# A spectral filter and a gated feed-forward on one core: x of two batches and the output weights loaded as plain f32 and cast on the engines, the opening's queues in a new order

## The chip, the core and the metric

The kernel runs on one core of a Trainium2 chip. The metric is device time in microseconds, the median of several executions. The core has five engines, each with a queue of its own that it works through in order: TensorE (PE in the profile; PEld is its weight load), VectorE (DVE), ScalarE (ACT), GpSimd (POOL) and SyncE (SP), which here only issues transfers. Transfers (DMAs) issued by SP or ACT move bytes as they are; those issued by POOL can change the type on the way, and the kernel before uses that to load f32 as f16. All of them run on the same 16 DMA engines.

## The reference

x has 8 batches of 3008 positions by 256 channels. Each channel of each batch is filtered in the frequency domain, then every position goes through a normalized, gated feed-forward of width 1536:

```python
X = np.fft.rfft(x, axis=1)
Y = X * (filt_r + 1j * filt_i)[None, :, :]
y = np.fft.irfft(Y, n=x.shape[1], axis=1)          # (8, 3008, 256)
x = y.reshape(24064, 256)
xn = x / np.sqrt(np.mean(x * x, -1, keepdims=True) + 1e-6) * rms_g
g = xn @ w_gate
out = (g / (1 + np.exp(-g))) * (xn @ w_val) @ w_out
```

All inputs and the output are f32; TensorE works on f16.

## The kernel before, in words

**The filter.** 3008 is 47 times 64; the transform is done in two steps. Positions are laid out as 94 partitions by 32 rows (r). Step one (`s1`, L139) multiplies with a 94 by 96 table `w1`, two rows of r at a time, 16 times a batch; the result goes to tile `a_sb` (one for each four calls, four slots) and by a store to `a_tmp` in DRAM, from which `load_a2` (L156) fetches it in another order. Step two (`s2`, L195) multiplies with the table `u`, then with the filter: for batches 0 and 1 by two DVE products straight from psum (L207 with `fr_sb`, L208 with `fi_sb`). `s2z` (L221) transforms back by `v1` and `v2` (made on the chip by `make_v`, L452), ACT evicts to `z_sb`, and each third call stores to `z_tmp`. `load_z2` (L240) fetches that in another order into the one slot of tag `z2`. `s3` (L247) is the last transform and takes the sums of squares on ACT (`junk`, L256); `s3r` (L260) makes rho from them on POOL; `s3n` (L271) normalizes on DVE into `n_sb`, stores that, and `load_xn` fetches it transposed as `xn`.

**Batch 0** takes shorter ways, so that TensorE starts early. `s1_first` (L163) computes step one with x as the stationary operand, four groups of eight rows, and leaves the result transposed in `at`, which borrows the slot of `z2`; `turn` (L183) turns it back into `a2` on TensorE, without the trip through DRAM. The first two chunks (`PRE` = 2) of normalized rows are turned on TensorE too (`turn_n`, L294, from `s3n_first`, L282), without a trip.

**The feed-forward** runs in units (`unit`, L337): for a chunk of 376 (batch 0) or up to 512 positions and one of 12 column blocks, two gate matmuls `pg`, two value matmuls `pv`, a Silu on ACT (L349), a DVE product to `hh` (L351), and three units later the projection `po` (`project`, L354). There are 50 chunks and 600 units. The work of the filter for later batches is dealt out to slots by a plan written by hand: `at(slot, f, ...)` puts a call behind the unit of that number.

**The opening.** All calls stand under a manual schedule: each engine works in the order of the code. POOL first issues four transfers of x of batch 0 (`load_x`, L130, f32 to f16 on the way) and the first of four pieces of the filters (`load_f`, L436: each piece is four transfers, each into every second of 64 partitions, half of them rows of 6 KB and half single rows of 1 KB); SP issues the tables. In a loop over the four groups of x follow `s1_first`, `make_v`, and, on SP, the other filter pieces, held back by a DVE memset (L510) into the columns that they fill. `copy_f` (L447) copies each filter piece to the other half of the partitions, the first time with DVE for `fr_sb`, else all on POOL. Then a loop over j has `turn(j)`, `s2(0, j - 2)` and `s2z(0, j - 4)` side by side. In it SP issues the first four feed-forward weight pieces (`load_w`, L476, 256 KB f32 each, staged in tag `xn`), and POOL issues x of batch 1, folds four pieces (`fold_w`, L482: times rms_g, to f16, columns reordered) and issues the first third of the output weights (`load_wo`, L488). Behind the loop come two loads of eight rows of `z2`, four more weight pieces, 12 calls of `s1` of batch 1, `s3` and `s3r` for the first two chunks, the last four calls of `s1`, `turn_n(0)`, four folds on DVE, `turn_n(1)`, the rest of `z2` and `load_a2(1)`; then the units.

Of the kernel before, what the change touches and what calls it, by code (L numbers as in the profile page):

```python
# [13 lines left out]
ALU = mybir.AluOpType  # L14
# [9 lines left out]
RP = 32  # L24
PX = 2 * M1
PY = 96
QZ = 4 * NS
# [4 lines left out]
def _make_tables():  # L32
# [32 lines left out]
    def rows_first(a):  # L65
        a = a.reshape(NS, 4, RP, P).transpose(2, 1, 0, 3)
        return np.ascontiguousarray(a.reshape(P, NS, P)).astype(f16)

    return (w1.reshape(PX, QZ).astype(f16), rows_first(u),
            w0.reshape(P, 1).astype(np.float32), t.reshape(QZ, PY).astype(f16),  # L70
# [4 lines left out]
def kernel(  # L75
# [12 lines left out]

    w1_np, u_np, w0_np, t_np, eye_np = _make_tables()
    w1_d = nc.inline_tensor(w1_np, name="w1tab").ap()  # L90
    u_d = nc.inline_tensor(u_np, name="utab").ap()
    w0_d = nc.inline_tensor(w0_np, name="w0tab").ap()
# [18 lines left out]
    v1_sb = glob.tile([P, NS, P], FP16)  # L111
    eye_sb = work.tile([P, 512], FP16, tag="hh", name="eye", bufs=5)[:, 0:P]
    w0_sb = glob.tile([P, 1], FP32)
# [16 lines left out]
    def load_x(b):  # L130
        v = st[b]
        v.x = []
        for g in range(4):
            xt = work.tile([PX, 8, D], FP16, tag="xt", name="xt", bufs=4)
            nc.gpsimd.dma_start(
                xt, x[b].rearrange("(p r) d -> p r d", r=RP)[:, ds(8 * g, 8), :])
            v.x.append(xt)

    def s1(b, i, eng):  # L139
        v = st[b]  # L140
        if i % 4 == 0:
            v.a = work.tile([QZ, 8, D], FP16, tag="a_sb", name="a_sb", bufs=4)
        ps = bank("psa")
        nc.tensor.matmul(ps[0:QZ, :], w1_sb, v.x[i // 4][:, ds(2 * (i % 4), 2), :],  # L144
                         start=True, stop=True)
        dst = v.a[:, ds(2 * (i % 4), 2), :]
        src = ps[0:QZ, :].rearrange("p (r d) -> p r d", r=2)
        if eng == 0:
            nc.scalar.activation(out=dst, in_=src, func=AXT.Copy)  # L149
        else:  # L150
            nc.vector.tensor_copy(out=dst, in_=src)
        if i % 4 == 3:
            nc.sync.dma_start(
                a_dram[b].rearrange("s c r d -> (s c) r d")[:, ds(8 * (i // 4), 8), :], v.a)

# [7 lines left out]
    def s1_first(g):  # L163
        v = st[0]
        if g == 0:
            t1 = work.tile([P, RP, D], FP16, tag="z2", name="at", bufs=1)
            v.at = t1.rearrange("p a b -> p (a b)")[:, 0:2 * NS * P].rearrange(
                "p (h s r c) -> p h s r c", h=2, s=NS, r=RP)
            v.a2 = work.tile([P, NS, D], FP16, tag="a2", name="a2", bufs=1)
        for i in range(2):  # L170
            for dh in range(2):
                ps = bank("psa")
                for r in range(4):
                    nc.tensor.matmul(ps[:, ts(r, QZ)], v.x[g][:, 4 * i + r, ts(dh, P)], w1_sb,
                                     start=(r == 0), stop=(r == 3))
                dst = v.at[:, dh, :, ds(8 * g + 4 * i, 4), :]
                src = ps[:, 0:4 * QZ].rearrange("p (r s c) -> p s r c", r=4, s=NS)
                if dh == 0:
                    nc.scalar.activation(out=dst, in_=src, func=AXT.Copy)
                else:  # L180
                    nc.vector.tensor_copy(out=dst, in_=src)

    def turn(j):  # L183
        v = st[0]
        ps = bank("psa")
        for e in range(2):
            for dh in range(2):
                k = 2 * e + dh
                nc.tensor.matmul(ps[:, ts(k, P)],
                                 v.at[:, dh, 2 * j + e, :, :].rearrange("p r c -> p (r c)"),  # L190
                                 eye_sb, start=(k == 0), stop=(k == 3))
# [101 lines left out]

    def turn_n(c):  # L294
        n = s3n_first(c)
        xn = work.tile([P, 2, 512], FP16, tag="xn", name="xn", bufs=9)
# [26 lines left out]
    for v in st:  # L323
        v.t12, v.y, v.xn = {}, {}, {}

# [71 lines left out]
    def at(slot, f, *args):  # L397
        plan.setdefault(slot, []).append((f, args))

    for c in range(PRE, RP // 4):  # L400
        k = 2 + 8 * (c - PRE)
        at(k, s3, 0, 2 * c, 2)
# [5 lines left out]
    for b in range(1, B):  # L408
        end = FIRST + UNITS * (b - 1)
        o_s1 = 44 if b == 2 else end - 118  # L410
        o_s2, p_s2 = (12, 3) if b == 1 else (end - 75, 2)
        o_s3 = 62 if b == 1 else end - 31
        if b > 1:
# [38 lines left out]
    def make_v(c):  # L452
# [6 lines left out]
        if k:  # L459
            nc.scalar.activation(out=v1_sb[:, 0, :], in_=pv[:, 0, :], func=AXT.Copy, scale=w0_sb)  # L460
        nc.scalar.activation(out=v1_sb[:, 4 * c + k:4 * c + 4, :], in_=pv[:, k:4, :],
                             func=AXT.Copy, scale=VSCALE)
        if c % 2 == 1:
            sl = ds(4 * c - 4, 8)
            v2 = work.tile([P, 8, P], FP16, tag="u", name="v2", bufs=3)
            v2_sb.append(v2)
            nc.vector.tensor_copy(out=v2[0:64], in_=v1_sb[64:P, sl, :])
            nc.vector.tensor_scalar(out=v2[64:P], in0=v1_sb[0:64, sl, :],
                                    scalar1=-1.0, scalar2=None, op0=ALU.mult)

# [17 lines left out]
    def load_wo(k):  # L488
        nc.gpsimd.dma_start(wo_sb[:, ts(k, 4), :],
                            moe_w_out.rearrange("(k p i) d -> k p i d", p=P, i=4)[k])  # L490

    with tc.manual_schedule():
        load_x(0)
        nc.sync.dma_start(w1_sb, w1_d)
        nc.sync.dma_start(u_sb, u_d)
        nc.sync.dma_start(eye_sb, eye_d)
        nc.sync.dma_start(w0_sb, w0_d)
        nc.sync.dma_start(t_sb, t_d)
        for dh in range(2):
            nc.sync.dma_start(g_sb[:, ds(dh, 1)], moe_rms_g[ds(dh * P, P)].unsqueeze(-1))  # L500
        nc.vector.memset(half_sb, -0.5)
        load_f(0, nc.gpsimd)
        for g in range(4):
            s1_first(g)
            if g < 3:
                make_v(2 * g)
                make_v(2 * g + 1)
            if g > 0:

                nc.vector.memset(fr_sb[0:1, 6 * g, 0:1], 0.0)  # L510
                load_f(g, nc.sync)
        copy_f(0)
        for j in range(15):
            if j < 12:
# [7 lines left out]
            if j == 6:  # L522
                load_w(4)
            if j == 10:
                load_x(1)
                for i in range(4):
                    fold_w(i, nc.gpsimd)
                load_wo(0)
        s2z(0, 11)
        load_z2(0, 0, 8)  # L530
        load_z2(0, 8, 8)
        load_w(4)
        for i in range(12):
            s1(1, i, i % 2)
        for c in range(PRE):
            s3(0, 2 * c, 2)
            s3(0, 2 * c + 1, 2)
            s3r(0, 2 * c, 2)
        for i in range(12, 16):
            s1(1, i, 1)  # L540
        load_wo(1)
        load_wo(2)
        turn_n(0)
        load_w(4)
        for i in range(4, 8):
            fold_w(i, nc.vector)
        turn_n(1)
        load_z2(0, 16, 16)
        load_a2(1)
        for i in range(8, 12):  # L550
            at(5, fold_w, i, nc.vector)

# [38 lines left out]
```

## Time and profile before

| what | us |
|---|---|
| median of 3 runs (904.06 to 905.67) | 904.35 |
| the profiled execution, whole | 903.57 |
| its span, first to last instruction | 901.7 |
| first gate matmul of the first unit | 60.97 |
| TensorE busy, whole span | 862.3 (96%) |
| first / last filter product of batch 0 (L207, L208) starts | 19.43 / 33.44 |
| last z store issued / landed | 35.32 / 42.4 |
| first `psy` matmul (L250) | 49.28 |

The views used below: *busy time of stretches* has for each stretch its length, the busy time of PE, PEld, DVE, ACT and POOL (with the number of instructions), the mean granted TensorE clock, the mean busy share of the 16 DMA engines and the GB/s that they moved. The *chain of waits* follows the work that ended last back from its end, here in order of time: start, length, and what ran or was waited for. The *timeline* has start, length, engine, line, operation, output and inputs; brackets hold the idle time before and what ended it. The *DMA view* cuts a stretch into 40 slices, with the GB/s moved in each.

### The profile page before, as it was taken

How to read it: one execution, taken by the hardware profiler on the slowest of the kernel's cores; microseconds unless marked ns; L12 is line 12 of the kernel's file. 1: busy time of each engine (PE TensorE's matmuls, PEld its weight loads, DVE VectorE, ACT ScalarE, POOL GpSimd, SP SyncE). 2: the span in 40 equal slices, each digit the busy share in tenths (PEclk: the TensorE clock that was granted, in tenths of full speed). 3: DMA queues.
4: the chain of work that ended last, by engine and by line, in shares of the span. 5: the costliest groups of instructions: out<-in, count | busy, mean ns of one | idle time of the engine just before them, and what ended most of it. 6: DMA issues, size and time to landing. Idle time of an engine off the chain costs nothing.

```text
span 901.7 us, 16399 instructions
## 1 busy us (share of the span) xinstructions
PE 862.3 (96%) x5528; PEld 549.6 (61%) x5528; DVE 645.6 (72%) x1025; ACT 640.1 (71%) x1455; POOL 336.5 (37%) x438
## 2 busy tenths in 40 slices
PE   5659999999999999999999999999999999999997
PEld 4326766666556655666556665566656665665655
DVE  4658887895588947697477965789477985865554
ACT  5546678777886778677886878867786775854543
POOL 3712104592245803285044821459033850500000
PEclk9859999999999999999999999999999999999999
DMA  9995766565436565354645554365653425260101
GB/s 211 238 257 124 167 156 212 122 145 130 144 101 143 128 146 170 99 108 129 163 146 129 138 123 151 106 131 145 146 159 100 97 78 117 77 130 24 42 29 45
DMA packets 140796, 117.30 MB, mean 130 GB/s; under 512 B 53960, under 2 KB 125256, under 8 KB 140712
## 3 DMA queue, kind: packets, MB, share of 16 engines
q1 hardware_dynamic: 136472, 102.36, 42.5%
q0 software_dynamic: 4240, 13.90, 8.6%
q8 instruction: 43, 0.70, 0.3%
q14 instruction: 41, 0.34, 0.1%
HBM read 56.96 MB, written 60.42 MB: 130 GB/s over the span
## 4 chain that ended last, share of the span: by engine, by line
PE 87%; ACT 4%; DMA 3%; DVE 2%; issue 2%; POOL 1%; ACTq 0%; SPq 0%; DVEq 0%; POOLq 0%
PE po L364 26%; PE pv L346 26%; PE pg L342 25%; PE psy L250 2%; PE psa L144 2%; ACT junk L256 2%; PE psz L229 2%; PE psp L200 2%; ACT sg L349 2%; DMA fi_sb<-in_filt_i_dram 1%; DMA z_tmp<-z_sb 1%; DMA z<-z_tmp 1%; DVE t L208 1%; DVE hh L351 0%; POOL fi_sb L450 0%
## 5 line engine op out<-in xcount | busy, mean ns | idle before, releaser
L351 DVE TENSOR_TENSOR hh<-pv,sg 128x512 f16<-128x512 f32 (+2 forms) x600 | 392.5, 658 | 219.8 <-ACT sg L349 128.3
L349 ACT ACTIVATE sg<-pg 128x512 f32<-128x512 f32 (+2 forms) x600 | 340.6, 568 | 193.8 <-PE pg L342 159.9
L364 PE MATMUL po<-wo_sb,hh 128*128 128x256 f16 (+2 forms) x2304 | 349.4, 272 | 0.2 <-DVE n_sb L276 0.2
L346 PE MATMUL pv<-xn,wv_sb 128*128 128x512 f16 (+2 forms) x1200 | 342.2, 367 | 4.4 <-ACT sg L349 3.8
L342 PE MATMUL pg<-xn,wg_sb 128*128 128x512 f16 (+2 forms) x1200 | 342.4, 367 | 0.6 <-DVE wg_sb L484 0.3
L364 PEld LDWEIGHTS <-hh 128*128 128x128 f16 (+2 forms) x2304 | 235.0, 104 | 102.4 <-DVE n_sb L276 0.5
L346 PEld LDWEIGHTS <-wv_sb 128*128 128x128 f16 x1200 | 117.5, 98 | 132.7 <-issue 6.3
L265 POOL TENSOR_SCALAR me<-ms 96x2 f32<-96x2 f32 (+1 forms) x120 | 26.0, 217 | 349.3 <-ACT junk L256 348.4
L342 PEld LDWEIGHTS <-wg_sb 128*128 128x128 f16 x1200 | 117.4, 98 | 14.1 <-issue 1.1
L217 POOL TENSOR_TENSOR pi<-pi,fi_sb 64x512 f32<-64x512 f32 x72 | 91.3, 1268 | 70.4 <-ACT pi L214 66.6
L256 ACT ACTIVATE junk<-psy 96x256 f16<-96x256 f32 x256 | 97.1, 379 | 20.9 <-PE psy L250 8.7
L218 POOL TENSOR_TENSOR qq<-pr,pi 128x512 f16<-128x512 f32 x72 | 91.6, 1272 | 10.2 <-DVE pi L216 4.4
L267 POOL TENSOR_TENSOR rho<-me,half_sb 96x2 f32<-96x2 f32 (+1 forms) x120 | 87.3, 728 | 10.0
L276 DVE TENSOR_TENSOR n_sb<-psy,rho 96x512 f16<-96x512 f32 x112 | 75.8, 677 | 0.0
L234 ACT ACTIVATE z_sb<-psz 128x512 f16<-128x512 f32 x96 | 57.3, 597 | 10.1 <-PE psz L232 5.8
L149 ACT ACTIVATE a_sb<-psa 96x512 f16<-96x512 f32 x94 | 55.4, 591 | 7.2 <-PE psa L144 3.5
L250 PE MATMUL psy<-z,t_sb 96*96 96x512 f16 x128 | 49.2, 389 | 7.8 <-DMA z<-z_tmp 7.8
L216 DVE TENSOR_TENSOR pi<-psp,fi_sb 64x512 f32<-64x512 f32 x72 | 49.9, 693 | 1.9
L215 DVE TENSOR_TENSOR pr<-psp,fr_sb 128x512 f32<-128x512 f32 x72 | 49.6, 689 | 0.6
L256 ACT ACTIVATION_READ_ACCUMULATOR junk<-psy 96x1 f32 x256 | 49.0, 191 | 0.0
L214 ACT ACTIVATE pi<-psp 64x512 f32<-64x512 f32 x72 | 42.4, 588 | 6.1
L144 PE MATMUL psa<-xt,w_sb 94*96 94x512 f16 x112 | 42.5, 399 | 3.0 <-DMA xt<-in_x_dram 2.8
(53 smaller groups left out, 382.6 us busy)
## 6 DMA issues: line engine op xcount, KB each, us to landing
out_dram<-o SPq DMA_DIRECT2D x70, 256.0 KB, 2.5
z_tmp<-z_sb SPq DMA_DIRECT2D x32, 384.0 KB, 2.3
xt<-in_x_dram POOLq DMA_DIRECT2D x32, 376.0 KB, 7.3
a_tmp<-a_sb SPq DMA_DIRECT2D x28, 384.0 KB, 3.6
a<-a_tmp SPq DMA_DIRECT2D x28, 384.0 KB, 5.5
z<-z_tmp SPq DMA_DIRECT2D x7, 1536.0 KB, 10.0
n_tmp<-n_sb SPq DMA_DIRECT2D x28, 384.0 KB, 3.0
out_dram<-o SPq DMA_DIRECT2D x14, 224.0 KB, 2.6
```

The costliest lines, as they stand in the source:

```text
L144: nc.tensor.matmul(ps[0:QZ, :], w1_sb, v.x[i // 4][:, ds(2 * (i % 4), 2), :], start=True, stop=True)
L217: nc.gpsimd.tensor_tensor(out=pi[64:P], in0=pi[64:P], in1=fi[64:P], op=ALU.mult)
L218: nc.gpsimd.tensor_tensor(out=qq, in0=pr, in1=pi, op=ALU.subtract)
L250: nc.tensor.matmul(ps[0:PY, :], t_sb, v.z2[:, ts(q, 2), :], start=True, stop=True)
L256: nc.scalar.activation(out=junk, in_=ps[0:PY, ts(i, D)], func=AXT.Square, scale=0.0625, accum_out=v.ms[:, ds(k + i, 1)])
L267: nc.gpsimd.tensor_tensor(out=rho, in0=me, in1=half_sb[:, 0:2 * pair], op=ALU.pow)
L276: nc.vector.tensor_tensor(out=v.n[:, ds(2 * (q % 4), 2), :], in0=ps[0:PY, :].rearrange("p (r d) -> p r d", r=2), in1=rho.unsqueeze(-1).to_ ...
L342: nc.tensor.matmul(pg[:, 0:w], wg_sb[:, dt_, ts(jt, P)], xn[:, dt_, 0:w], start=(dt_ == 0), stop=(dt_ == 1))
L346: nc.tensor.matmul(pv[:, 0:w], wv_sb[:, dt_, ts(jt, P)], xn[:, dt_, 0:w], start=(dt_ == 0), stop=(dt_ == 1))
L349: nc.scalar.activation(out=sg[:, 0:w], in_=pg[:, 0:w], func=AXT.Silu)
L351: nc.vector.tensor_tensor(out=hh[:, 0:w], in0=pv[:, 0:w], in1=sg[:, 0:w], op=ALU.mult)
L364: nc.tensor.matmul(po[0:n, ts(s4 % 2, D)], hh[:, ds(s4 * wb, n)], wo_sb[:, jt, :], start=(jt == 0 and s4 % 2 == 0), stop=(jt == JT - 1 and ...
```

## The change

x of batch 0 is loaded by eight transfers from SP and eight from ACT as plain f32 into columns 8 to 23 of the filter tiles `fr_sb` and `fi_sb`, and cast into `xt` by DVE (partitions 64 to 110) and POOL (partitions 0 to 46; of the last group ACT casts three eighths). For that the two halves of each position pair lie 64 partitions apart, with a table `wh` for `s1_first`, zeros between. x of batch 1 is loaded by SP as plain f32, each part split into partitions 0 to 63 and 64 to 93: groups 0 and 1 into the slot of `z2`, group 2 into two slots of `n_sb`, group 3 into two of the four slots of `a_sb`; POOL casts three groups, DVE the last. The output weights go by SP into slots of `xt`, and POOL casts them. `at` now borrows the slots of `wg_sb` and `wv_sb`. The filters, all on SP, have no memset ahead of them any more; three pieces come behind the loop over g. The stores of `a_sb` of groups 0 to 2 of batch 1 are put off to a list `dma_a`. `z2` is loaded by 4, 4, 8 and 16 rows, the third with two `load_wo` around it. Four folds move from POOL to DVE ahead of the first `s1` of batch 1; the other eight, the last four `s1`, `turn_n(1)`, the last part of `z2` and `load_a2(1)` move into the first slots of the plan. `make_v2`, taken out of `make_v`, runs once on POOL and twice on DVE. Some slots of batches 0 and 1 move by 1 to 4.

```diff
+    def load_x0(g):
+        stage = (fr_sb, fi_sb)[g % 2][:, ds(8 + 8 * (g // 2), 8), :]
+        src = x[0].rearrange("(m q r) d -> q m r d", q=2, r=RP)
+        for q, eng in ((0, nc.sync), (1, nc.scalar)):
+            for m0, n in ((0, 32), (32, M1 - 32)):
+                eng.dma_start(stage[ds(64 * q + m0, n)], src[q, ds(m0, n), ds(8 * g, 8), :])
+        st[0].stage.append(stage)
+
+    def cast_x0(g):
+        xt, stage = st[0].x[g], st[0].stage[g]
+        k = 8 if g < 3 else 5
+        nc.vector.tensor_copy(out=xt[64:PH], in_=stage[64:PH])
+        nc.gpsimd.tensor_copy(out=xt[0:M1, 0:k, :], in_=stage[0:M1, 0:k, :])
+        if k < 8:
+            nc.scalar.activation(out=xt[0:M1, k:8, :], in_=stage[0:M1, k:8, :], func=AXT.Copy)
+
+    def load_x1(g):
+        v = st[1]
+        if g < 2:
+            if g == 0:
+                v.half = work.tile([P, RP // 2, D], FP32, tag="z2", name="x1a", bufs=1)
+            parts = [v.half[:, ds(8 * g, 8), :]]
+        else:
+            parts = [work.tile([P, 4, D], FP32, tag=("n_sb", "a_sb")[g - 2], name="x1b",
+                               bufs=(2, 4)[g - 2]) for _ in range(2)]
...
+        for k, part in enumerate(parts):
+            for p0, p1 in ((0, 64), (64, PX)):
+                nc.sync.dma_start(part[p0:p1], src[p0:p1, ds(8 * g + n * k, n), :])
+
+    def cast_x1(g, eng):
...
+        for k, part in enumerate(v.stage[g]):
+            eng.tensor_copy(out=xt[:, ts(k, n), :], in_=part[0:PX])
...
     def load_wo(k):
-        nc.gpsimd.dma_start(wo_sb[:, ts(k, 4), :],
-                            moe_w_out.rearrange("(k p i) d -> k p i d", p=P, i=4)[k])
+        stage = work.tile([P, 4, D], FP32, tag="xt", name="wos", bufs=4)
+        nc.sync.dma_start(stage, moe_w_out.rearrange("(k p i) d -> k p i d", p=P, i=4)[k])
...
+    def cast_wo(k):
+        nc.gpsimd.tensor_copy(out=wo_sb[:, ts(k, 4), :], in_=wo_stage[k])
...
-        load_x(0)
-        nc.sync.dma_start(w1_sb, w1_d)
+        nc.sync.dma_start(tabs[:, ds(P, QZ)], wh_d)
+        load_x0(0)
         nc.sync.dma_start(u_sb, u_d)
         nc.sync.dma_start(eye_sb, eye_d)
+        load_x0(1)
         nc.sync.dma_start(w0_sb, w0_d)
+        load_x0(2)
+        load_x0(3)
+        load_f(0, nc.sync)
...
         for g in range(4):
+            cast_x0(g)
             s1_first(g)
+            if g == 2:
+                make_v2(0, nc.gpsimd)
+                make_v2(1, nc.vector)
...
-                nc.vector.memset(fr_sb[0:1, 6 * g, 0:1], 0.0)
-                load_f(g, nc.sync)
+        for c in range(1, 4):
+            load_f(c, nc.sync)
+        load_w(4)
+        load_x1(0)
         copy_f(0)
+        make_v2(2, nc.vector)
         for j in range(15):
...
             if j == 6:
-                load_w(4)
-            if j == 10:
-                load_x(1)
-                for i in range(4):
-                    fold_w(i, nc.gpsimd)
-                load_wo(0)
+                load_x1(1)
         s2z(0, 11)
-        load_z2(0, 0, 8)
-        load_z2(0, 8, 8)
-        load_w(4)
-        for i in range(12):
-            s1(1, i, i % 2)
+        for g in range(2):
+            cast_x1(g, nc.gpsimd)
+        load_x1(2)
+        load_z2(0, 0, 4)
+        load_z2(0, 4, 4)
+        for i in range(4):
+            fold_w(i, nc.vector)
+        dma_a = []
+        for i in range(8):
+            s1(1, i, i % 2, dma_a)
+        load_x1(3)
+        cast_x1(2, nc.gpsimd)
         for c in range(PRE):
             s3(0, 2 * c, 2)
             s3(0, 2 * c + 1, 2)
             s3r(0, 2 * c, 2)
+        load_wo(0)
+        load_w(4)
+        load_wo(1)
+        load_w(4)
+        load_z2(0, 8, 8)
+        load_wo(2)
+        for i in range(8, 12):
+            s1(1, i, 1, dma_a)
+        for f in dma_a:
+            f()
+        n0 = s3n_first(0)
+        turn_n(0, n0)
+        cast_x1(3, nc.vector)
+        n1 = s3n_first(1)
+        for k in range(3):
+            cast_wo(k)
         for i in range(12, 16):
-            s1(1, i, 1)
-        load_wo(1)
-        load_wo(2)
-        turn_n(0)
-        load_w(4)
-        for i in range(4, 8):
-            fold_w(i, nc.vector)
-        turn_n(1)
-        load_z2(0, 16, 16)
-        load_a2(1)
-        for i in range(8, 12):
-            at(5, fold_w, i, nc.vector)
+            at(2 + (i - 11) // 2, s1, 1, i, 0)
+        at(4, load_a2, 1)
+        at(4, load_z2, 0, 16, 16)
+        at(2, turn_n, 1, n1)
+        for i in range(4, 12):
+            at((0, 0, 1, 1, 4, 4, 5, 5)[i - 4], fold_w, i, nc.vector)
```

## The prediction

> **What bounds the kernel now.** I read the busy time of stretches first. From 71 us on TensorE leads (48.08 of 49 us, then 772.82 of 781.7); the opening, up to the first gate matmul at 61 us, fills half of TensorE while the DMA share is 0.95.
>
> ```profile
> 0.00:61.00 61.00, 31.77 (x245) 21.93 (x246) 34.31 (x62) 29.53 (x64) 30.02 (x34) 0.79 0.95 236
> 61.00:71.00 10.00, 9.60 (x60) 5.80 (x58) 6.98 (x13) 7.74 (x19) 1.26 (x2) 0.89 1.16 246
> 71.00:120.00 49.00, 48.08 (x351) 34.58 (x349) 42.42 (x81) 33.85 (x94) 8.44 (x14) 1.00 0.56 131
> ```
>
> So the change is worth what it does to the start of the units. The chain of waits (start, length) names the links: the first filter piece, its copy on POOL, DVE's 24 products, the last z store, the z load, the normalizing, the folds.
>
> ```profile
> 5.14 12.69 DMA fi_sb<-in_filt_i_dram
> ...
> 17.97 2.12 POOL fi_sb L450
> ...
> 33.52 0.61 DVE t L208
> ...
> 35.32 7.07 DMA z_tmp<-z_sb
> ...
> 42.94 6.29 DMA z<-z_tmp
> ...
> 53.45 0.68 DVE a_sb L151
> 54.13 1.21 DVE n L287 x2
> ...
> 61.17 0.63 PE pg L342 x2
> ```
>
> DVE's own timeline shows that it keeps the order of the code: the second normalizing (L287, 59.18) had its rho at 55.4, yet stood behind four folds that waited for their loads.
>
> ```profile
> 51.65 2.48 DVE L151 CAST a_sb<-psa 96x512 f16<-96x512 f32 x4 [9.46 <-PE psa L144]
> 54.05 1.27 DVE L287 TENSOR_TENSOR n<-psy,rho 96x512 f16<-96x512 f32 x2
> 56.08 1.01 DVE L307 CAST xn<-psn 128x384 f16<-128x384 f32 x1 [0.76 <-PE psn L300]
> 56.90 0.63 DVE L484 TENSOR_SCALAR wg_sb<-stage,g_sb 128x512 f16<-128x512 f32 x1
> ```
>
> Last the DMA view, in 40 slices: up to 12 us (0.3 us each) and from 12 to 42 us (0.75 us each).
>
> ```profile
> GB/s 0 0 0 0 0 14 53 259 61 389 369 410 369 410 314 262 230 225 218 205 191 137 82 82 193 126 195 113 167 128 225 171 196 198 197 224 221 221 226 246
> ```
> ```profile
> GB/s 189 306 254 213 221 219 254 232 243 269 249 236 229 255 240 261 234 234 283 345 371 363 350 414 367 145 85 180 197 213 180 212 273 251 272 262 259 243 249 221
> ```
>
> Loads into all 128 partitions (u at 2.7 to 4.2 us, weights at 26 to 30) run at 345 to 414 GB/s: I use 390. The filters, each piece into one half of the partitions (15 to 25 us), run at 220 to 270: I use 240. Casting x loads show about 220, counted in f16, so 440 of source, but on a queue of their own.
>
> **Start of the products.** x of batch 0 is 3.08 MB, u and the first filter piece 0.79 each. Bytes flow from 2.1 us. Group 0 (both halves side by side at 390) ends at 4.1. u then shares with ACT's queue, to 8.1; SP's half of group 1 to 10.1; SP's halves of groups 2 and 3 are alone, 385 KB at 240, to 11.7 and 13.3; the filters end at 16.6, against 17.8 now. Issues: ACT's eight take 8 by about 0.45 = 3.6 us (weight issues 0.38 to 0.46) after its 1.28 us table load, in the time in which it now waits 6.07 for its first psum; SP has them free too. If an issue had to wait for a landing, as L153's did (2.9 us in SP's waits), ACT's evictions would start late.
>
> The casts are new. DVE: 2048 elements by the fr copy (1536 in 0.95) 1.27 us; by the 1-per-cycle eviction row (512 in 0.69) 2.8. POOL: by its copy (1536 in 1.46) 1.95; by its fold (512 in 2.04) 8.2. I take the copies, whose access is the same, and 0.65 more on POOL while DVE copies (2.11 against 1.46). make_v2 on POOL, two of 1024: 0.84 (DVE's rows) to 8.2; taken 1.95. So POOL, after 0.5 to landing: cast 1 from 10.6 to 13.2, cast 2 to 15.8, make_v2 to 17.7, cast 3 (1280, the rest on ACT, about 0.8) to 19.6. From the last s1_first to the first product is now 15.24 to 19.43, 4.2 us: the products (L207 and L208) start at 23.8, **4.4 later**; 24 of them at the trace's 0.60 us spacing end at 38.2. That the filters land earlier is of no use here: POOL has become the last to arrive. memsets, tables, t, g and w1 are small and hidden behind these loads.
>
> **The z trip.** Pieces 1 to 3 of the filters wait for the casts (their columns hold the stage): 16.6 to 27.1 at 240 with a pause; four weight pieces (1.05 MB) to 29.8; x1's first groups 3.2 us each at 240, a z store 1.0 each: all four stores are through by about 40.5, landed at 41 against 42.4. Had the products ended earlier, the queue would still hold z until then: it covers 3 of the 4.4 us. z2's slot is free, since POOL's casts of x1 (1.95 each) end at about 40. x1's third group is issued ahead of the z load: to 43.7; four rows instead of eight by the z row (1536 KB in 10.0 us, about 200 GB/s) 1.0. First psy at 45.5 instead of 49.28, **3.8 earlier**.
>
> **The new wait.** Tag a_sb has four slots. Tiles of s1 groups 0 and 1 (stores now put off to the end of the list) and the two stages of x1's last group fill them. The third group's evictions (i = 8 to 11, all DVE) need a slot: the stages are freed by a cast that stands behind them on DVE, so they wait for group 0's store. On SP that store stands behind x1's last group, three wo pieces, eight weight pieces and z2's next eight rows. Queue on from 44.7: z rows 4 to 7 to 45.7, x1 48.9, wo 49.6, weights 52.3, wo 53.0, weights 55.7, z2 57.7, wo 58.4, store 59.4, landed at **60**. It is in order that this queue runs: the last z store, 384 KB, took 7.07 us to land behind other loads, where over the whole run such a store takes 2.3 (the page's list of DMA issues). Behind the held eviction on DVE stand both normalizings and everything of the units; TensorE, ACT and POOL wait for them. Then 4 evictions take 2.5 (the 51.65 row), and from the start of n to both halves of xn written it is 3.0 (54.05 to 57.09): units start at 65.5 against 60.97, **+4.5**. So the 3.8 us that the z trip gains are given back, and more: the start of the units no longer hangs on the z load, but on how much the SP queue has to move before that store.
>
> **First units.** DVE has cast x1 (2 by 0.63), n 1.27, 8 folds by 0.68, turn_n(1) 1.0 and 6 products by 0.55 before the seventh product: 12.3 us after the start, now 9.3 (70.31); in the time before, the third n (1.29) follows at once and now comes slots later, under TensorE's cover, so of the 3.0 us I count **+2.5**. TensorE's moved work (4 s1 by 0.38, 8 small matmuls 1.0) lies inside. The casts of wo on POOL (3 by 0.97) lie in 10 us of idle POOL; folds 0 to 3 on DVE (2.7 instead of 8.2 on POOL) in the z trip. What is late next: load_a2 at slot 4 needs some 11 us, slot 16 follows some 14 later; without these 3 us TensorE stalls by as much.
>
> Sum +7.0: span 901.7 to 908.7, its execution 903.57 to 910.6. That execution is 0.78 under the median 904.35, so I forecast **911.4**. Its own range is 905 to 917: the store may land from 56 us (the casts and make_v2 at their DVE-like lower prices, small z rows faster) to 64 (make_v2 on POOL at the fold's price), and the DVE part may be 1 to 4.
>
> The Trainium skill, "SBUF — State Buffer", section "Door 1: The DMA port swizzle", says that DMA rate goes by how many of 16 ports the partitions reach, and partitions 0 to 63 reach eight. By that rule x1's [0:64] and [64:94] pieces get at most half of 436, an estimate of 218 GB/s; four groups would cost 1.2 us more than in my sum. The trace agrees for the filters (240 against 390); no run here shows it for x1.
>
> **Rivals.** (1) **x1 at the full rate.** The slow filter loads may be slow for their 1 KB rows, not for their half of the partitions; against it, the casting load showed no better than 440. Then each x1 group takes 2.0, 4.8 in all: store landed at 55.2, units at 60.7, -0.3 + 2.5 = +2.2: 906.5.
> (2) **The slot does not hold DVE**: the other side. The store lands early, or the third group gets another slot. For it: two queues, deferred stores and folds out of the way are worth much. Against: four slots, five live tiles, DVE in order. Place: first eviction of i = 8. With T the first psy, unheld evictions run from T + 2.4 (49.28 to 51.65) to T + 4.9, units at T + 7.9 = 53.4: -7.6 + 2.5 = -5.1, **899**. It decides from a landing at 53 us down: there units start at 58.5 and the sum is zero.
> (3) **POOL casts at the fold's 4 ns an element**: cast 3 ends at about 36, products at 55, two casts of x1 hold z2's slot until 61, first psy 63.5, units at 83: +25, 929. Against: the fold reads with a stride, the cast doesn't.
>
> **Chances.** Forecast 0.52, rival 1 0.12, rival 2 0.29, rival 3 0.07. A measurement here tells 0.2% (1.8 us) from no change. Faster: 0.28 of rival 2, 0.02 of rival 1: 0.30. Same: 0.01, 0.06, and 0.02 of the forecast: 0.09. Slower: 0.61. Range 896 to 920: it leaves out some 0.07 of rival 2 and 0.10 above.
>
> **What would show it.** Right: DVE's first L151-type eviction of i = 8 idle until a DMA of a_tmp, ten us or more; psy at 44 to 47; first product at 22 to 25; x1 pieces at 220 to 260 GB/s. Wrong: DVE evicting straight behind psy, units before 56. A POOL cast far from 2 us, or the last z store landing after 44, breaks the terms before it.

## The result, and the profile after

The changed kernel takes 935.48 us (median of 4 runs, 933.47 to 936.78) against 904.29 beside it: 1.034 times as long, 95% interval 1.0318 to 1.0361. I had said 911.4, at most 920. Its profiled execution has a span of 933.6 us, 31.9 more than before.

The starts of some units (the first gate matmul of each, L392 now) say where the time went:

| first matmul of unit | 0 | 6 | 54 | 60 | 66 | 96 | 599 |
|---|---|---|---|---|---|---|---|
| before, us | 61.0 | 67.3 | 128.6 | 135.7 | 142.5 | 175.3 | 894.3 |
| after, us | 79.9 | 88.4 | 151.5 | 158.6 | 172.5 | 207.1 | 926.1 |
| difference | 18.9 | 21.1 | 22.9 | 22.9 | 30.0 | 31.8 | 31.8 |

So 18.9 us are lost ahead of the first unit, 4.0 in the next 54 units and 8.9 between units 54 and 96; from there on the two kernels keep pace. Busy time of stretches, after (columns as in the part before): the opening keeps TensorE busy for 31.64 of 79.9 us (before: 31.77 of 61), and from 151.5 to 215.6 TensorE stands for 6.4 us, where the same units left 0.4 us before (54.60 of 55.00 busy from 129 to 184). The same work also keeps TensorE busy for 3.1 us longer: the granted clock, 1.00 on both sides of it, is 0.50 from 165.5 to 172.3, around the longest stand. The last line is of the kernel before, for units 54 to 102.

```profile
0.00:10.00 10.00, 0.47 (x7) 0.47 (x8) 3.11 (x4) 0.00 (x0) 5.63 (x7) 1.00 0.84 205
10.00:20.00 10.00, 4.64 (x45) 3.69 (x42) 4.25 (x6) 5.04 (x10) 3.94 (x3) 1.00 1.03 190
0.00:79.90 79.90, 31.64 (x232) 22.22 (x233) 42.47 (x59) 29.00 (x63) 38.66 (x30) 0.81 0.92 232
...
151.50:215.60 64.10, 57.67 (x377) 38.43 (x375) 45.19 (x85) 43.16 (x126) 24.34 (x40) 0.95 0.64 152
165.50:172.30 6.80, 4.87 (x17) 2.77 (x18) 0.55 (x1) 2.85 (x10) 1.58 (x4) 0.50 0.53 165
...
129.00:184.00 55.00, 54.60 (x375) 37.34 (x373) 44.55 (x84) 42.95 (x126) 24.26 (x40) 1.00 0.67 169
```

The chain of waits, after (start, length, what):

```profile
5.85 9.21 DMA fi_sb<-in_x_dram
15.18 1.90 POOL xt L157
...
24.74 2.14 POOL xt L157
...
30.73 4.84 DMA fi_sb<-in_filt_i_dram
...
52.57 7.92 DMA x1b<-in_x_dram
60.50 5.77 DMA stage<-in_moe_w_val_dram
66.34 8.28 DMA a_tmp<-a_sb
75.36 1.87 DVE a_sb L198 x3
77.23 1.21 DVE n L338 x2
78.86 1.03 ACT xn L355
79.93 0.79 PE pg L392 x2
```

x0's second group lands at 15.06, the z load has left the chain, and the last link is the store of group 0 of `a_sb`. DVE's timeline shows the same link from the other side: the evictions of i = 8 to 11 follow 20.71 us of standing, ended by that store.

```profile
74.75 2.48 DVE L198 CAST a_sb<-psa 96x512 f16<-96x512 f32 x4 [20.71 <-DMA a_tmp<-a_sb]
77.15 1.27 DVE L338 TENSOR_TENSOR n<-psy,rho 96x512 f16<-96x512 f32 x2
```

POOL's timeline has the casts of x0 (L157) and `make_v2` (L518, L519):

```profile
15.18 1.89 POOL L157 CAST xt<-fi_sb 47x2048 f16<-47x2048 f32 x1 [5.70 <-DMA fi_sb<-in_x_dram]
17.88 1.89 POOL L157 CAST xt<-fr_sb 47x2048 f16<-47x2048 f32 x1 [0.81 <-DMA fr_sb<-in_x_dram]
19.83 1.92 POOL L518 COPY v<-v_sb 64x1024 f16<-64x1024 f16 x1
21.83 2.85 POOL L519 TENSOR_SCALAR v<-v_sb 64x1024 f16<-64x1024 f16 x1
24.74 2.13 POOL L157 CAST xt<-fi_sb 47x1280 f16<-47x1280 f32 x1
```

A cast takes 1.89 us, as predicted (1.95); the data is late, and `make_v2` holds the last cast back. On DVE the last `make_v2` (L518, L519 at 30.00) stands right ahead of the first product, whose psum TensorE has written by 30.8:

```profile
30.00 1.57 DVE L518 COPY v<-v_sb 64x1024 f16<-64x1024 f16 x1
31.59 1.59 DVE L519 TENSOR_SCALAR v<-v_sb 64x1024 f16<-64x1024 f16 x1
33.21 0.69 DVE L258 TENSOR_TENSOR t<-psp,fr_sb 128x512 f16<-128x512 f32 x1
```

ACT's timeline shows one more thing that I had counted at nothing. Its eight issues of x0 do not go out in 3.6 us: four are through by 4.96, the others stand until earlier transfers have landed, and the table load that comes first of ACT's own work, free of any data, starts at 13.82.

```profile
0.74 1.10 ACTq L150 DMA_DIRECT2D fr_sb<-in_x_dram  x2
1.88 3.08 ACTq L150 DMA_DIRECT2D fi_sb<-in_x_dram  x2
6.67 1.12 ACTq L150 DMA_DIRECT2D fr_sb<-in_x_dram  x2
12.07 1.71 ACTq L150 DMA_DIRECT2D fi_sb<-in_x_dram  x2
13.82 1.28 ACT L230 ACT_TABLE_LOAD   x1 [13.82 <-DMA fr_sb<-in_x_dram]
```

SP's waits have the same: 2.6, 1.8 and 3.2 us of L150's issues stand behind landings of `u_sb`, `tabs` and `fr_sb`. The trace shows why: the program tells the landings of SP's and ACT's transfers by eight semaphores in all, taken in turn, and an issue stands until the transfer that last used its semaphore has landed. So at most eight are out, and each queue waits for the other's transfers too: ACT's fourth issue goes out at 4.63, when its own first load has landed (4.61), and its fifth at 6.67, when SP's first load of x has (6.65).

The loss past unit 54 shows in TensorE's timeline: batch 1's first `psy` stands for its z load, which SP issues at 157.16 (before: 127.03).

```profile
167.43 0.66 PE L301 MATMUL psy<-z,t_sb 96*96 96x512 f16 x1 [5.17 <-DMA z<-z_tmp]
```

### The profile page after: what moved, and what is told of

Its sections match the earlier page's. It is cut to its first block, busy times and chain, and to the rows that moved or that the text cites. A ratio compares the mean times of both kernels' runs of the same rounds, so it can differ in the third digit from the quotient of the medians.

```text
span 933.6 us, 16457 instructions
## 1 busy us (share of the span) xinstructions
PE 867.3 (93%) x5528; PEld 551.9 (59%) x5528; DVE 659.4 (71%) x1030; ACT 642.3 (69%) x1458; POOL 345.4 (37%) x434
## 3 DMA queue, kind: packets, MB, share of 16 engines
q10 hardware_dynamic: 312, 1.54, 0.8%
## 4 chain that ended last, share of the span: by engine, by line
PE 85%; DMA 7%; ACT 4%; issue 2%; DVE 1%; SPq 1%; POOL 1%; ACTq 0%; DVEq 0%; POOLq 0%
PE po L414 26%; PE pv L396 25%; PE pg L392 25%; PE psy L301 3%; PE psa L191 2%; PE psz L280 2%; PE psp L251 2%; ACT junk L307 2%; ACT sg L399 1%; DMA z<-z_tmp 1%; DMA fi_sb<-in_x_dram 1%; DMA a_tmp<-a_sb 1%; DMA x1b<-in_x_dram 1%; DMA x1a<-in_x_dram 1%; DMA stage<-in_moe_w_val_dram 1%
## 5 line engine op out<-in xcount | busy, mean ns | idle before, releaser
L392 PE MATMUL pg<-xn,wg_sb 128*128 128x512 f16 (+2 forms) x1200 | 343.5, 368 | 2.3 <-DMA xn<-n_tmp 1.0
L392 PEld LDWEIGHTS <-wg_sb 128*128 128x128 f16 x1200 | 117.5, 98 | 15.8 <-issue 2.4
L307 ACT ACTIVATE junk<-psy 96x256 f16<-96x256 f32 x256 | 97.0, 379 | 25.8 <-PE psy L301 13.3
L269 POOL TENSOR_TENSOR qq<-pr,pi 128x512 f16<-128x512 f32 x72 | 91.6, 1273 | 10.6 <-DVE pi L267 5.0
```

Source lines behind the costliest of these rows:

```text
L269: nc.gpsimd.tensor_tensor(out=qq, in0=pr, in1=pi, op=ALU.subtract)
L307: nc.scalar.activation(out=junk, in_=ps[0:PY, ts(i, D)], func=AXT.Square, scale=0.0625, accum_out=v.ms[:, ds(k + i, 1)])
L392: nc.tensor.matmul(pg[:, 0:w], wg_sb[:, dt_, ts(jt, P)], xn[:, dt_, 0:w], start=(dt_ == 0), stop=(dt_ == 1))
```

## The experiments

My theory after this reading had three parts: x0's plain loads make the opening late, the slot of `a_sb` holds DVE, and batch 1's chain has lost its margin. Each had a rival. Four kernels (the freed slot, the loads alone, `make_v2` on DVE, s3 three slots later) were executed once each, on one chip, with the kernel before at 905.24; for the others the ratio of the means is given with its interval.

**One slot for DVE (the hold).** x1's last group is staged elsewhere, as four parts of two rows:

```diff
-            parts = [work.tile([P, 4, D], FP32, tag=("n_sb", "a_sb")[g - 2], name="x1b",
-                               bufs=(2, 4)[g - 2]) for _ in range(2)]
+            parts = [work.tile([P, 4, D], FP32, tag="n_sb", name="x1b", bufs=2) for _ in range(2)] \
+                if g == 2 else [work.tile([P, 512], FP32, tag=tag, name="x1c", bufs=bufs).rearrange(
+                    "p (r d) -> p r d", r=2) for tag, bufs in (("sg", 3), ("sg", 3), ("o3", 2), ("o3", 2))]
```

> x1's last group is staged in slots of sg and o3 (four parts of two rows) instead of two slots of a_sb; stores and all else as in the changed kernel. Theory (the slot holds DVE): the first eviction of i = 8 no longer waits 20.7 us for group 0's store but runs right behind psy; units start about 8 us after the first psy instead of 21.4, so near 66.5 instead of 79.9, and the time falls by 9 to 13 us, to 922 to 926. Rival (the queue of weight pieces is late anyway and the units wait for folds and output weights instead): units start earlier but stall, and the time falls by less than 5 us.

Measured 920.28 us. DVE's evictions of i = 8 to 11 now wait for TensorE alone, and units start at 65.86 instead of 79.93, 7.7 us behind a `psy` that stayed where it was (58.19). The hold is shown, and worth 14 to 15 us, more than the 9 to 13 expected. DVE's timeline of this run:

```profile
60.68 2.48 DVE L199 CAST a_sb<-psa 96x512 f16<-96x512 f32 x4 [6.34 <-PE psa L192]
63.08 1.27 DVE L339 TENSOR_TENSOR n<-psy,rho 96x512 f16<-96x512 f32 x2
```

**x0's way of loading.** The loads alone, one after the other, with nothing of the reference computed, each timed to its landing:

> A kernel that only loads: no part of the reference is computed and the output is not its. Six stages, one after the other, of four loads of eight rows each: (a) x of batch 0 as the change loads it, halves on SP and ACT; (b) the same, all on SP; (c) the lower half alone; (d) x of batch 1 as the change loads it, partitions 0 to 63 and 64 to 93; (e) 128 partitions; (f) the casting load of 94 partitions. Theory of the prediction (the two halves side by side run at the full rate, one half alone at 240 GB/s): (a) 3.08 MB in 8 us, (c) 1.54 MB in 6.4 us, (d) in 12.8 us, (e) 4.19 MB in 11 us, (f) in 8 us of 3.08 MB read. Rival (pieces of 32 and 15 partitions are slow themselves, also side by side): (a) and (b) at 190 to 220 GB/s, 14 to 16 us, as the profile of the changed kernel suggests with 190 to 205 GB/s over its first 20 us.

Busy time of stretches, one line for each of the six ways (columns here: length, DVE, POOL, clock, DMA share, GB/s written, so that the casting load's counts f16):

```profile
9.43:26.24 16.81, 3.51 (x3) 0.00 (x0) 1.00 0.82 183
26.60:46.53 19.93, 0.00 (x0) 0.00 (x0) 1.00 0.85 155
46.91:58.39 11.48, 0.00 (x1) 0.00 (x0) 1.00 0.77 134
58.76:74.93 16.17, 0.00 (x0) 0.00 (x0) 1.00 0.84 191
75.31:87.67 12.36, 0.00 (x0) 0.00 (x0) 1.00 0.85 339
88.29:98.62 10.33, 0.00 (x0) 2.17 (x4) 1.00 0.80 149
```

In order: x0's way from SP and ACT; the same from SP alone; its lower half alone (1.54 MB); x1's way; four loads of 128 partitions (4.19 MB); POOL's casting loads of 94 partitions. The same 3.08 MB of x take 16.8 or 16.2 us plain and 10.3 by the casting load. Both halves side by side run at 183 GB/s, not at the 339 of the full-width load: the step "both halves side by side at 390" is refuted. Standing issues are not what makes them slow: the lower half alone and x1's way are eight transfers each, none of which stood, and they run at 134 and 191; and the DMA engines are as busy at 183 GB/s (0.82) as at 339 (0.85). The full-width load differs from x1's in the size of its transfers too (1 MB each against 0.5 and 0.25), so what the width alone does is not divided from that.

In the kernel, x0 loaded as before, the rest as changed:

```diff
-        nc.sync.dma_start(tabs[:, ds(P, QZ)], wh_d)
-        load_x0(0)
+        load_x(0)
+        nc.sync.dma_start(w1_sb, w1_d)
...
-            cast_x0(g)
```

> The kernel after, with x of the first batch loaded as before (POOL's casting loads of 96 partitions, products against w1), nothing of it cast by an engine; x1, the output weights, make_v2(0) and the folds stay as changed. Theory (x0's plain loads are what makes the start late): the first product starts near 20 us instead of 33.2, psy near 45 instead of 58.4, and the time falls by the same 9 to 14 us, to 921 to 927 us, if group 0's a_tmp store moves with psy. Rival (the slot hold does not move with it, because x1's loads, now queued behind, still land at the same time and the units wait for group 0's store near 66 us): psy earlier but units within 3 us of 79.9, time 932 to 936 us.

Measured 920.89 us, ratio to before 1.0178 (1.0163 to 1.0193). First product at 21.98, first `psy` at 44.84 (after: 33.21 and 58.44), units at 68.0. The theory held. The hold moved along with it (20.03 us of standing, 20.71 in the changed kernel), which confirms it once more; DVE's timeline:

```profile
62.85 2.48 DVE L198 CAST a_sb<-psa 96x512 f16<-96x512 f32 x4 [20.03 <-DMA a_tmp<-a_sb]
```

It undoes loads and casts together; the traces divide them. Here x0 has landed at 16.26. In the changed kernel it has at about 22.7, which is when SP issues the table `w1` (22.69), held back by that landing. So some 6.4 of the 11.2 us at the first product are later landing, and the rest is casts and what stands around them.

**ACT's blocked issues, or the rate.** All of x0's loads from SP (`(0, nc.sync), (1, nc.sync)` in `load_x0`):

> The kernel after, with all sixteen of x0's plain loads issued by SP instead of eight by SP and eight by ACT. Theory A (the loads' own rate sets the start; the loads alone took 16.8 us from two queues and 19.9 from one): first product 2 to 4 us later than 33.2, time 937 to 940 us. Theory B (ACT's issues, which stand until 13.8 us in front of its casts, set the start): first product earlier than 33.2 by 1 us or more, time 932 to 934 us.

Measured 934.48 us, ratio 1.0327 (1.031 to 1.0345), not to be told from the changed kernel's. In the profile ACT's table load is at 0.75, the first product at 30.98 (2.2 earlier) and units at 77.5: theory B's sign, and its time but for half a microsecond. Of the 2.2 us, 1.1 is `make_v2` on DVE right ahead of the product, which takes 2.1 us instead of 3.2; so ACT's blocking is worth 1 to 2 us at the start. The loads alone had taken 3 us longer from one queue; here the landing that releases `w1` comes at 22.42, no later than with two queues. The 9 us that are left to the 21.98 of the run above are the loads' rate together with the casts.

**`make_v2` on POOL.** Its first call on DVE (`make_v2(0, nc.vector)`):

> The first make_v2 runs on DVE instead of POOL. It cost POOL 1.92 and 2.85 us ahead of the last cast of x of batch 0, where 1.95 were predicted; DVE needs 0.41 and 0.42. Theory (POOL's order holds back the products): the last cast starts about 4 us earlier, the products at 29.5 to 31 instead of 33.2, and the time falls by 1.5 to 4 us. Rival (x's last group has only just landed, or the queue holds z back): no more than 1 us.

Measured 934.24 us, first product at 34.47, units at 81.0: the rival's result, or 0.2 us more (935.48 to 934.24), but not for its reason alone. POOL does stand for landings now, 1.14 us ahead of the last cast of x0 and 1.99 ahead of the first filter copy; yet that cast starts at 21.70, 3.0 us earlier, much as the theory had it. What did not follow is DVE: both calls of `make_v2` now stand ahead of its own last cast, which starts at 26.71 instead of 23.82, and TensorE waits for that one:

```profile
26.71 1.23 DVE L156 CAST xt<-fi_sb 47x2048 f16<-47x2048 f32 x1
28.08 1.44 PE L225 MATMUL psa<-tabs,xt 111*128 111x96 f16 x16 [3.84 <-DVE xt L156]
```

The edit moved the wait from one engine to the other. What the 4.77 us on POOL cost is not shown by it.

**Batch 1's margin.** First s3 alone, three slots later (`o_s3 = 66`):

> Batch 1's last transforms start three slots later (o_s3 66 instead of 63); nothing else. In the changed kernel the distance from load_z2(1) to the first s3 of batch 1 shrank from 13 slots to 10 while that load still takes 10 us, and TensorE stands 5.2 us at psy around 162 us; six units from 60 to 66 took 13.9 us instead of 6.8. Theory (the margin of the hand-written slots): the stall falls by 3 slots of about 1.25 us, the time by 3 to 5 us (to 930.5 to 932.5 from 935.5). Rival (the SP queue is late anyway, or the transposed loads for unit 96 become the next stall): under 1 us.

Measured 936.31 us. The stand at unit 66 goes, and the units 54 to 120 take 90.8 us against 91.0 (before: 82.2): the next consumer, the transposed rows for unit 96, becomes the stall. TensorE's timeline:

```profile
206.03 0.60 PE L392 MATMUL pg<-xn,wg_sb 128*128 128x512 f16 x2 [2.71 <-DMA xn<-n_tmp]
```

Moving the consumer alone gains nothing. The z load in two halves of 16 rows, in the same slot:

```diff
-        at(k + (4 if b < 2 else 6), load_z2, b)
+        if b == 1:
+            at(k + 4, load_z2, b, 0, 16)
+            at(k + 4, load_z2, b, 16, 16)
+        else:
+            at(k + 6, load_z2, b)
```

> The kernel after, with the second batch's z load (load_z2(1), of 32 rows, 10 us from issue to landing) made as two loads of 16 rows in the same slot of the order. Theory (the 9 us lost between units 54 and 120 come from this load's landing, which s3 of batch 1 waits for): the first half lands some 4 us earlier, units 54 to 120 take 84 to 87 us instead of 91.0, time 929 to 932 us. Rival (the loss is the late order of the whole batch's s3, as moving s3 alone did not gain): 90 to 91 us, time 934 to 936 us.

Measured 930.53 us, ratio 1.028 (1.0264 to 1.0295): 86.3 us from unit 54 to 120, where 82.2 were needed before. The wait is shown, and a little less than half of the loss is left. Both parts of it shrank: between units 54 and 102 TensorE stands for 3.9 us instead of 6.4, 1.33 of them for this load, and is busy for 55.5 instead of 57.7 us, at a granted clock of 1.00 throughout.

**All three undone at once**, the other parts of the change kept (small z loads, folds on DVE, turn ahead of the last `s1`, x1 and output weights plain):

> Three edits together: x1's last group staged in other tiles so that a_sb's four slots are free, x0 loaded as before, and load_z2(1) made as two loads. Theory (the three losses are the start, the hold and batch 1's z load, and they add up): psy near 45, units from 53 to 55 instead of 79.9, time 900 to 908 us. Rival (the early start runs into another wait, x1's landings, since POOL's queue now holds x0's casting loads ahead of them): units from 60 or later, time 910 us or more.

Measured 905.77 us (902.41 to 909.15), ratio 1.0014 (0.9997 to 1.003). Units start at 52.2, a little ahead of the 53 to 55 expected and 8.8 us ahead of the kernel before; at unit 54 the lead is 4.4, at 102 it is 1.0. So the three losses are the whole of the 31 us within the interval, and what the reorder gains in the opening is spent again in the units. The rows below are of one execution each, and not each is a typical one: that of three undone (902.41) is the fastest of ten, that of the earlier chain (905.04) lies 1.8 us above its median, that of the small z loads (904.38) is the slowest of eleven. They show where the time goes; which kernel is faster, the medians say.

| first matmul of unit | 0 | 54 | 120 | 599 |
|---|---|---|---|---|
| before | 61.0 | 128.6 | 210.8 | 894.3 |
| three undone | 52.2 | 124.2 | 209.8 | 893.3 |
| and the chain two slots earlier | 53.7 | 130.3 | 212.5 | 896.0 |
| before, small z loads | 60.3 | 129.4 | 211.6 | 895.2 |
| before, small z loads, turn first | 55.3 | 129.4 | 211.7 | 895.2 |
| three undone, s2 of batch 1 denser | 52.9 | 123.8 | 205.9 | 889.4 |

**Where the lead goes.** First the chain two slots earlier (s3 by one): `s1(12)` to `s1(15)` in slots 0, 0, 1, 1, `load_a2` in 2, `o_s2` 14, `o_s3` 62.

> The three edits of the run before (a_sb's slots free, x0 loaded as before, load_z2(1) in two), and batch 1's chain two slots earlier: s1(12) to s1(15) in slots 0, 0, 1, 1, load_a2 in slot 2, o_s2 14 and o_s3 62. Theory (the 3 us in which PE stood between units 54 and 102 of the run before come from the chain's four slots of delay): units 54 to 120 take 83 to 84 us instead of 85.6, time 902 to 904 us. Rival (PE is busy for 97 to 100 per cent of the stretch from the first unit on, so the work moved into it costs its own time): within 1 us of 905.8.

Measured 903.28 us, ratio 0.9989 (0.9976 to 1.0001): no difference to the kernel before that can be told. Units 54 to 120 are back at 82.2 us, but the first `s2` of batch 1 comes before its data, and units 12 to 16 take 11.5 us, where the run before had 4.6. TensorE's timeline:

```profile
77.48 0.58 PE L252 MATMUL psp<-a,u_sb 128*128 128x256 f16 x2 [5.23 <-DMA a<-a_tmp]
```

The landing of `a2` of batch 1 is a limit that an earlier start runs into. Two runs start from the kernel before. The first has only its first z load made as two of 4 rows:

> The kernel before, with the first batch's first z load of 8 rows made as two of 4 rows, nothing else. Theory (psy at 49.28 waits for the landing of eight rows, and four rows land some 2 us earlier): psy near 47, units near 59, time 902 to 903.5 us. Rival (x1's casting loads fill the DMA engines then, so that the smaller load lands no earlier, or the earlier start is eaten by PE's busy units): within 1 us of 904.4.

Measured 903.04 us, ratio 0.9981 (0.9972 to 0.999). `psy` comes at 48.57 instead of 49.28 and units at 60.3, and by unit 54 the profiled execution is no longer ahead (129.4 against 128.6). The clock takes the gain there: at the start of the units it is 0.50 for 5.4 us, in the kernel before for 2.3. Busy time of stretches, the kernel before and this run, from the first unit until the clock is 1.00:

```profile
61.00:63.30 2.30, 2.30 (x11) 1.14 (x9) 1.01 (x1) 2.27 (x3) 0.00 (x0) 0.51 1.07 256
...
60.30:65.70 5.40, 5.40 (x20) 2.65 (x18) 2.57 (x4) 4.51 (x10) 0.00 (x0) 0.50 1.13 251
```

Half speed for 3.1 us more is 1.5 us of work, an estimate, and 1.6 is what the first 30 units take longer (37.6 against 36.0). Whether the other executions had it too is not recorded; this one was the slowest. The same with the first turn ahead of the last `s1`, the second turn in slot 2 and folds 4 to 7 in slots 0 and 1:

> The kernel before with the change's order behind the z trip alone and no plain load of x: two z loads of 4 rows first, the first n and its turn ahead of s1(12) to s1(15), the second turn in slot 2, folds 4 to 7 in slots 0 and 1. Theory (the 11.7 us from psy to the first unit fall to 8, and psy comes 2 us earlier): units at 54 to 56 instead of 61.0, of which a half to two thirds is given back by unit 102 as in the run with three edits, time 901 to 903.5 us. Rival (all of it is given back, since PE is the bound from the first unit on): 903.5 to 906 us.

Measured 904.52 us, ratio 0.9999 (0.9989 to 1.0009). Units start at 55.3, and 129.4 at unit 54 is the time of the run above: the rival's result, though by another way than it said. TensorE stands 2.44 us for `a2` at 74.82, and units 0 to 12 take 16.3 us instead of 13.3.

**A version that beats both.** The three edits with the s2 steps of batch 1 begun at slot 16, when `a2` is there, but 8/3 slots apart, so that they end where they did before the change:

```diff
-            k = o_s2 + p_s2 * j
+            k = o_s2 + (8 * j // 3 if b == 1 else p_s2 * j)
-        o_s3 = 63 if b == 1 else end - 31
+        o_s3 = 62 if b == 1 else end - 31
```

> The three edits together (a_sb's slots free, x0 loaded as before, load_z2(1) in two), with batch 1's s2 steps 8/3 slots apart instead of 3, so that they begin at slot 16 as there and end four slots earlier, and o_s3 62. Theory (units from 52, and no stand of PE between units 54 and 102, since batch 1's z load is issued at the slot where the kernel before has it): units 54 to 120 take 82.5 to 84 us instead of 85.6, time 901.5 to 904 us and below the kernel before. Rival (what is saved there is spent earlier, in denser units 16 to 52): 904.5 to 906.5 us.

Measured 898.75 us (898.48 to 903.77) against 903.88 beside it, ratio 0.996 (0.9945 to 0.9975): faster than the kernel before by 0.4% of the means (three of its ten executions lie near 903), below the 901.5 to 904 expected, and faster by 4% than the changed one. Units 54 to 120 take 82.1 us, and the lead at unit 120 is 4.9. Busy time of stretches of this run, up to the first unit, over units 0 to 30, and over the first of these alone:

```profile
0.00:52.90 52.90, 31.08 (x232) 21.29 (x233) 35.24 (x53) 28.68 (x62) 26.39 (x26) 0.86 0.93 242
52.90:91.80 38.90, 37.81 (x251) 25.33 (x251) 34.63 (x66) 26.69 (x67) 8.94 (x13) 0.93 0.81 230
...
52.90:58.30 5.40, 5.39 (x23) 2.88 (x23) 5.40 (x11) 3.72 (x6) 1.30 (x2) 0.50 1.04 387
```

Units 0 to 30 took 36.0 us before and take 38.9 here, with TensorE busy for 37.81 of them (35.12 before). Of these 2.7 us some 1.5 are the clock, by the same estimate as above: it is 0.50 for the first 5.4 us here and was for 2.3. The rest is work that was done ahead of the units and now lies in them.

## Why the prediction fell short, step by step

The mechanism was right, and so was its side: DVE held by a slot until group 0's store has landed, the units behind it, the z load off the path. The sizes of its terms were not, and one loss of 8.9 us was not in the sum at all.

| step | predicted | measured |
|---|---|---|
| cast of x0's second group on POOL starts | 10.6 | 15.18 |
| x0 landed | 13.3 | about 22.7 |
| last cast of x0 ends | 19.6 | 26.87 |
| first product / first `psy` | 23.8 / 45.5 | 33.21 / 58.44 |
| group 0's store landed | 60 | 74.62 |
| first unit, against before | +4.5 | +18.9 |
| first units | +2.5 | +4.0 |
| batch 1, units 54 to 96 | 0 | +8.9 |
| span | +7.0 | +31.9 |

**Start of the products: the step that failed, by 9.4 us.** "Group 0 (both halves side by side at 390)" and all that followed took the rate of a load into 128 partitions for two loads into a half each. The first 20 us move 205 and 190 GB/s, and by themselves these loads make 183. The Trainium skill, "SBUF — State Buffer", section "Can I just issue two DMAs to hit both halves?", says no: two at once were only 6% faster than one. The run of the loads agrees that two halves do not make the full width, 183 GB/s against 339; it differs in the factor, 183 side by side against 134 for one half alone, 1.37 times. The prediction drew on this page for x1 and did not apply it to x0. By the page's factor on my 240 for a half, an estimate of 254 GB/s, x0 would take 12.1 us instead of 7.9; alone it took 16.8, so that the 240, read from the filters, was too much for it as well (134 for the half alone).

By the end of the last cast 7.3 of the 9.4 us have come. The other 2.1 are a second miss in this step: the 4.2 us from the last `s1_first` to the first product were taken from the kernel before, where DVE is through with `make_v2` ahead of the last evictions and the first product waits for TensorE alone. Now a `make_v2` of 3.2 us stands right ahead of it on DVE, and the stretch is 6.3 us.

**"SP has them free too": the second part of it.** The prediction named the case, that an issue has to wait for a landing, and gave it no price. It happened on both queues, behind the eight semaphores that they share; on ACT it is worth 1 to 2 us.

**make_v2 on POOL** was mis-sized, 4.77 us (1.92 and 2.85) against 1.95, and held the last cast back from its data's landing at about 22.7 to 24.74. The run with it on DVE does not show what that cost, because the wait moved to DVE.

**The z trip.** From the last product's end to `psy` it was 7.3 us in the sum and is 10.8: four rows of z, issued at 51.67 right behind x1's third group, took 6.7 us to land, where 1.0 was counted for them and 3.2 for x1's bytes ahead. That is 3.5 us of the miss (from the first product: 25.2 us against 21.7). More than half of the shortening that the sum counted did come: 15.2 us before, 10.8 now.

**The new wait.** From `psy` to the first unit 20.0 us were predicted, and 21.5 measured: the queue that the store stands in came out well, on a start that was 13 us late. It did so although one term in it is half its size: each of the three output weight pieces is 0.52 MB of f32, 1.3 us at 390, and the sum took 0.7; put right, `psy` to the store's landing would be 16.4 us instead of 14.5, and it measured 16.2. Without the hold it is 7.7 (predicted 7.9). Rival 2 thus describes the run with the slot freed, but its price, 899, was reckoned from a `psy` at 45.5.

**First units**, +4.0 by unit 54 where 2.5 were counted to the seventh product: 2.2 of it lies by unit 6. Some 0.7 of it, an estimate, is the clock: 0.50 for the first 3.7 us of the units, until 83.6, where the kernel before had 2.3.

**Batch 1, not in the sum.** I checked the margin of `load_a2` and slot 16, and not that of the slots behind them: `o_s2` moves by four slots and `o_s3` by one. The z load is issued 7.2 us later against the units (30.1 later, the units 22.9), takes 10.2 to land, and what waits for it moves by one slot, some 1.2 us. TensorE stands, and some 3.1 of the 8.9 us are not the stand but the clock of 0.50 around it.

These five add up: 9.4 at the products, 3.5 on the z trip, 1.5 from `psy` to the first unit, 1.5 in the first units and 8.9 in batch 1 are 24.8 of the 24.9 us between +7.0 and +31.9.

**Rivals 1 and 3** are refuted: x1's way runs at 191 GB/s, not at the full rate and under the 220 to 260 that the prediction named as well, and the casts are near 2 us. A sign that the prediction had named for a broken term before the hold came too: the last z store was to land by 44, and it was issued at 48.85.

What stays open: why a half-width load is so slow, its width or the size of its transfers; how much `make_v2` costs in either place; what sets how long the clock stays at 0.50 when the units start; and what parts the two levels of the fastest version, seven of ten executions near 898.5 to 899.5 and three near 903.

## What to carry to other kernels

Before a casting load is replaced by a plain one plus casts, time the plain one by itself in its own shape, partitions and queue: the full-width rate does not carry over to two half-width loads. When a temporary borrows a slot from a tag in use, count the live tiles of that tag and look which engine's next write waits, and behind what its release is queued. Before work is moved to another engine, look what it then stands ahead of. When a chain in a hand-made plan is moved, check the margin of every later link, and win time back by denser steps after the data is there rather than by an earlier first step.

## What the runs showed of the hardware, unexpected

The casting load of 94 partitions read its 3.08 MB of f32 in 10.3 us, faster than the plain loads of the same bytes into two halves (16.2 to 19.9); at the 339 GB/s of the full-width load they would take 9.1, an estimate. Issuing a transfer is not free of the transfers ahead of it, though that is the program's doing: with its eight semaphores taken, the ninth transfer of SP and ACT together stands. In the run of the loads SP alone issues its ninth at 30.34, when the first has landed (30.32). ACT's first own instruction came at 13.82 instead of 0.75 by this. The two parts of `make_v2`, 64 by 1024 of f16, took POOL 1.92 and 2.85 us, and DVE 0.41 and 0.42 for the same shapes (1.57 and 1.59 in its next call). The granted clock is 0.50 or 1.00 in these traces from the units on, and a stand of TensorE can cost more than its length: around that of 5.2 us for batch 1's z load (from 162.3) it was 0.50 from 165.5 to 172.3, and with the z load split, where that stand is 1.33 us, it stayed at 1.00. At the start of the units it stayed at 0.50 for 2.3 us in the kernel before and for 5.4 in the run with small z loads, though their units start within 0.7 us of each other; so an earlier start does not explain it.
